# A gated linear attention with an ELU feed-forward layer: the scan input of span 1 loaded ahead of q and k of span 0, and its scan moved behind that of span 0

## The chip, the core and the metric

The kernel runs on one core of one Trainium2 chip. The metric is device time in microseconds (us). The engines are PE (TensorE: matmuls, with its weight loads listed as PEld), DVE (VectorE), ACT (ScalarE), POOL (GpSimd) and SP (SyncE, which here issues the transfers). Each engine works through its own list of instructions in order and waits at an instruction whose inputs are not there yet.

## The reference

```
state = zeros((B, H, D, D))
for t in range(S):
    state = alpha[:, :, t, :, None] * state + einsum('bhd,bhe->bhde', k[:, :, t], v[:, :, t])
    y[:, :, t] = einsum('bhd,bhde->bhe', q[:, :, t], state)
x = y.transpose(0, 2, 1, 3).reshape(B * S, H * D)
h = x @ w_in
g = where(h > 0, h, exp(minimum(h, 0)) - 1)
out = g @ w_out
```

B = 4, H = 8, S = 768, D = 48; w_in is 384 x 2048 and w_out 2048 x 384. All of it is float32 to the caller.

## The kernel before, in words

Time is cut into spans of 128 steps, 6 for each of the 4 batches, 24 in all. Within a span the recurrence becomes matrix products: a running product P of alpha (the scan, with a row of ones in front), its inverse R (by logarithm and exponential), k divided and q multiplied by P, then score, state and output matmuls. Two spans make one block of 256 tokens for the feed-forward layer, whose weights are split into a high and a low part by the engines while the first spans run. After the first 60 us or so the weights are ready and the rest is a steady alternation of spans and feed-forward matmuls.

The order of all work is written by hand: a table of tokens, START, is read from left to right and each token emits its instructions; each engine then holds its own instructions in that order. The tokens that matter here, for span i:

- LA.i loads the alpha part ("a") of the span, 128 x 516 numbers, 258 KB; LB.i loads its k and q, 128 x 1024 numbers, 512 KB, into the same tile `qka`. Both are issued by SP (lines 179 and 183). LV.i loads v, F.f a piece of the weights, L.i all of a later span.
- SC.i is the scan on DVE (line 209): P from a. LN.i and EX.i, both on ACT (lines 218 and 223): R = exp(-ln P). EX also reads out an accumulator, a short instruction of its own.
- KA.i (line 231): k times R, kept in `qka`. It needs EX.i and LB.i; for span 0 it runs on DVE. KB.i (line 236): R = P times R, on DVE for span 0 and on POOL for span 1; it overwrites the R that KA.i reads. KC.i (line 241, DVE): (R - 2) times k, which ends the preparation of k.
- SQ.i (line 258): q times P, on POOL for span 0 and on DVE for span 1. It needs SC.i and LB.i.
- TP.i (line 282, PE): four transposes of k, behind KC.i. KN.i (line 311, ACT) copies them out. S.i (line 346, PE): scores from k and SQ.i's result. U.i (line 392, PE): state update from KN.i's result. UA.i (line 409), UC.i (line 442), UP.i (line 418), MK.i (line 363), YL.i and Y.i (lines 453 and 497), XH.i (line 512) finish the span.
- X.n issues n matmuls on constant data (line 126); 16 of them stand ahead of TP.0.
- DA, DB, DC (lines 581, 587, 593, DVE), WH (line 619, ACT) and WP (lines 628 and 516, PE) split a pair of weights.

The lines on which the steps rest:

```
nc.sync.dma_start(out=qtile(i)[:, 2 * NP * W:], in_=qka[i, :, 2 * NP * W:QW])            # LA
nc.sync.dma_start(out=win[i]["t"][:, 0:2 * NP * W], in_=qka[i, :, 0:2 * NP * W])         # LB
nc.vector.tensor_tensor_scan(out=P..., data0=t[:, 2 * NP * W:], data1=first..., ...)     # SC
eng(KAV, i).tensor_tensor(out=d["kt"], in0=d["kt"], in1=d["R"], op=ALU.mult)             # KA
eng(KBV, i).tensor_tensor(out=d["R"], in0=pw(i), in1=d["R"], op=ALU.mult)                # KB
nc.vector.scalar_tensor_tensor(out=d["kt"], in0=d["R"], scalar=-2.0, in1=d["kt"], ...)   # KC
eng(SQV, i).tensor_tensor(out=st[:, 0], in0=d["q"], in1=pw(i), op=ALU.mult)              # SQ, i < 6
KAV, KBV, SQV = (0, 1, 2, 3, 10), (0, 3, 5, 6), (1, 2, 3, 5)   # spans on DVE; the others on POOL
```

Of the kernel before, what the change touches and what calls it, by code (L numbers as in the profile page):

```python
# [14 lines left out]
B, H, S, D = 4, 8, 768, 48  # L15
# [29 lines left out]


START = """
LA.0 LB.0 SC.0 LN.0 EX.0 LA.1 KA.0 KB.0 LB.1 SC.1 X.2 LV.0 LN.1 X.2 KC.0 F.2 SQ.0 EX.1 F.0 TP.0 KN.0 S.0 U.0
SQ.1 UA.0 KA.1 KB.1 MK.0 L.2 KC.1 UC.0 YL.0 LV.1 TP.1 PC.0 Y3.0 Y.0 KN.1 DA.0 PC.1 LV.2 DB.0 L.3 F.4 S.1 SC.2
U.1 XH.0 F.6 DC.0 UP.1 LN.2 XP.0 EX.2 KA.2 SQ.2 MK.1 UA.1 F.5 WH.0 WP.0 YL.1 F.1 F.3 UC.1 Y3.1 KB.2 SC.3 KC.2  # L50
WH.2 XL.0 PC.2 LN.3 DA.2 EX.3 SQ.3 Y.1 DB.2 KA.3 XH.1 TP.2 WP.2 DC.2 KB.3 KN.2 DA.1 DB.1 XP.1 KC.3 U.2 XL.1
# [916 lines left out]
```

## Time and profile before

| | |
|---|---|
| median of 3 runs | 504.81 us (504.31 to 505.99) |
| the profiled execution | 504.17 us |
| its span in the profile | 502.5 us |
| busy share of the span: PE, PEld, DVE, ACT, POOL | 98%, 95%, 77%, 58%, 26% |
| mean granted clock of TensorE | 0.999 |

Times in the profile count from the span's start, so the profiled execution's own time is its span and some 1.7 us around it. In a row of the timeline the first number is the start, the second the duration, then the engine, the line, the operation and its operands; brackets give the engine's idle time before it and what ended that. A row of transfers gives the tensor, the issuing queue, how many, the size of each and the time from issue to landing.

### The profile page before, as it was taken

The numbers are of one execution on the slowest core, as the hardware profiler recorded it, in microseconds if no ns is written. First come the engines' busy times: TensorE is split into PE (matmuls) and PEld (weight loads), VectorE is DVE, ScalarE is ACT, GpSimd is POOL, SyncE is SP. The second block draws the span as 40 slices with busy tenths as digits, with TensorE's granted clock in tenths as the row PEclk, the third lists the DMA queues.
The fourth block names the chain that finished last, engine by engine and source line by source line (L and its number), as shares of the span: only waits on it lengthen the run. The fifth ranks groups of instructions, "written<-read, shape, count | busy, mean of one in ns | idle before, by whom it ended". The sixth has DMA issues, their size and how long they took to land.

```text
span 502.5 us, 13254 instructions
## 1 busy us (share of the span) xinstructions
PE 492.4 (98%) x5404; PEld 476.0 (95%) x5404; DVE 386.6 (77%) x807; ACT 289.5 (58%) x689; POOL 129.4 (26%) x111
## 2 busy tenths in 40 slices
PE   7999999999999999999999999999999999999996
PEld 3789999999999899999999999999999999999996
DVE  6999999989998579769869969769969978344321
ACT  3656786456460677646745756647755755454432
POOL 4125566443320302501501501501501500000000
PEclk9999999999999999999999999999999999999999
DMA  8999324222521145226135145234332321110001
GB/s 311 412 411 382 91 95 165 64 59 100 190 59 64 57 130 178 65 83 219 54 119 178 48 119 182 63 112 172 82 112 97 95 76 44 56 42 8 3 33 36
DMA packets 22403, 61.13 MB, mean 122 GB/s; under 512 B 2880, under 2 KB 9792, under 8 KB 22336
## 3 DMA queue, kind: packets, MB, share of 16 engines
q1 hardware_dynamic: 22048, 59.83, 35.4%
q8 instruction: 44, 0.72, 0.6%
q10 hardware_dynamic: 288, 0.39, 0.2%
q14 instruction: 23, 0.19, 0.1%
HBM read 53.53 MB, written 4.72 MB: 116 GB/s over the span
## 4 chain that ended last, share of the span: by engine, by line
PE 96%; DVE 2%; ACT 1%; issue 1%; ACTq 0%
PE o L706 40%; PE h L655 40%; PE y L458 4%; PE y L453 2%; PE q L374 2%; PE q L330 2%; PE u L392 1%; PE sc L346 1%; PE wp L126 1%; PE y L497 1%; PE tp L282 1%; DVE kn L292 0%; PE yl L453 0%; PE wd L628 0%; DVE st L358 0%
## 5 line engine op out<-in xcount | busy, mean ns | idle before, releaser
L655 PE MATMUL h<-xt,w 128*128 128x256 f32 x1728 | 215.0, 282 | 0.0
L655 PEld LDWEIGHTS h<-xt,w 128*128 128x128 f32 x1728 | 209.3, 188 | 1.8
L706 PE MATMUL o<-w,gh 128*128 128x384 f32 x768 | 199.3, 341 | 0.6 <-ACT gh L679 0.6
L706 PEld LDWEIGHTS o<-w,gh 128*128 128x128 f32 x768 | 136.9, 188 | 1.6 <-ACT gh L679 0.8
L706 PE MATMUL o<-w,gl 128*128 128x384 f32 x384 | 130.0, 339 | 0.1
L679 ACT CAST gh<-h 128x512 fp32r<-128x512 f32 x96 | 55.9, 583 | 79.6 <-DVE h L673 39.3
L692 DVE TENSOR_TENSOR gl<-h,gh 128x512 fp32r<-128x512 f32 x96 | 65.5, 687 | 35.5 <-ACT gh L679 34.2
L292 DVE STREAM_TRANSPOSE kn<-qka 32x128 f32<-32x128 f32 x288 | 87.0, 302 | 4.5
L663 ACT ACTIVATE r<-h 128x512 f32<-128x512 f32 x96 | 57.0, 595 | 47.2 <-PE h L655 40.7
L673 DVE SCALAR_TENSOR_TENSOR h<-r,h 128x512 f32<-128x512 f32 x96 | 64.6, 689 | 16.9 <-ACT r L668 16.1
L706 PEld LDWEIGHTS o<-w,gl 128*128 128x128 f32 x384 | 72.1, 188 | 0.4 <-DVE gl L692 0.4
L231 POOL TENSOR_TENSOR qka<-qka,R 128x512 f32<-128x512 f32 x19 | 26.1, 1375 | 164.6 <-DVE gl L692 127.6
L668 ACT ACTIVATE r<-r 128x512 f32<-128x512 f32 x96 | 59.4, 631 | 0.7
L261 POOL TENSOR_TENSOR st<-qka,P 64x512 f32<-64x512 f32 x36 | 42.8, 1189 | 21.7 <-DVE P L209 16.2
L358 DVE TENSOR_TENSOR st<-q,mask 64x256 f32<-64x256 f32 x72 | 30.4, 422 | 12.0 <-ACT vs L409 9.2
L209 DVE TENSOR_TENSOR_SCAN P<-qka,first 128x516 f32<-128x516 f32 x24 | 30.6, 1275 | 1.6 <-DMA qka<-in_qka_dram 1.2
L236 POOL TENSOR_TENSOR R<-P,R 128x512 f32<-128x512 f32 x20 | 24.2, 1211 | 27.3 <-DVE qka L231 25.9
L218 ACT ACTIVATE R<-P 128x512 f32<-128x512 f32 x24 | 15.2, 632 | 27.8 <-DVE P L209 27.8
L411 DVE TENSOR_TENSOR vs<-vs,q 48x192 f32<-48x192 f32 x30 | 10.5, 350 | 19.1 <-PE q L330 16.9
L511 ACT ACTIVATE y<-y 128x128 fp32r<-128x128 f32 x20 | 5.5, 275 | 30.0 <-PE y L458 26.6
L639 POOL TENSOR_TENSOR w<-spare,w 128x768 fp32r<-128x768 f32 x7 | 15.8, 2256 | 26.0 <-ACT w L619 13.9
L611 ACT ACTIVATE ck<-ck,lim 128x384 f32<-128x384 f32 x32 | 20.6, 644 | 0.1
(101 smaller groups left out, 425.7 us busy)
## 6 DMA issues: line engine op xcount, KB each, us to landing
qka<-in_qka_dram SPq DMA_DIRECT2D x22, 770.0 KB, 6.5
raw<-in_wgt_dram SPq DMA_DIRECT2D x16, 768.0 KB, 12.3
ck<-in_wgt_dram SPq DMA_DIRECT2D x32, 384.0 KB, 3.2
vs<-in_vv_dram SPq DMA_DIRECT2D x36, 192.0 KB, 4.3
out_dram<-ot SPq DMA_DIRECT2D x22, 192.0 KB, 1.9
vs<-in_vv_dram SPq DMA_DIRECT2D x6, 384.0 KB, 11.6
xt<-y SPq DMA_DIRECT2D x40, 48.0 KB, 2.3
qka<-in_qka_dram SPq DMA_DIRECT2D x2, 512.0 KB, 5.0
```

Source lines behind the costliest of these rows:

```text
L209: nc.vector.tensor_tensor_scan(out=P.rearrange("p n w -> p (n w)"), data0=t[:, 2 * NP * W:], data1=first.rearrange("p n w -> p (n w)"), in ...
L231: eng(KAV, i).tensor_tensor(out=d["kt"], in0=d["kt"], in1=d["R"], op=ALU.mult)
L261: eng(SQV, i).tensor_tensor(out=st[r, a], in0=d["q"][r], in1=pw(i)[r], op=ALU.mult)
L292: nc.vector.transpose(out=kn[32 * t:32 * t + 32, :, 32 * g:32 * g + 32], in_=d["kt"][32 * g:32 * g + 32, :, 32 * t:32 * t + 32])
L358: nc.vector.tensor_tensor(out=d["st"][r, a, :, c * C:(c + 1) * C], in0=d["s4"][a][o], in1=mask[o].unsqueeze(1).broadcast_to([64, NP, C]), ...
L655: nc.tensor.matmul(h[:, f, :], lhsT=t[:, wi, ws], rhs=x[:, c, xi, :], start=(f == 0 and k == 0), stop=(k == 8), skip_group_check=True)
L663: nc.scalar.activation(out=r, in_=d["h"], func=AF.Relu, scale=-1.0)
L668: nc.scalar.activation(out=d["r"], in_=d["r"], func=AF.Exp, scale=-1.0)
L673: nc.vector.scalar_tensor_tensor(out=d["h"], in0=d["r"], scalar=-1.0, in1=d["h"], op0=ALU.add, op1=ALU.max)
L679: nc.scalar.copy(out=gh, in_=d["h"])
L692: nc.vector.tensor_tensor(out=gl, in0=d["h"], in1=d["gh"].bitcast(F32), op=ALU.subtract)
L706: nc.tensor.matmul(o[:, 0:DM], lhsT=gt[:, f, ms], rhs=t[:, wi, f * DM:f * DM + DM], start=(j == 0 and f == 0 and k == 0), stop=(j == NJ - ...
```

## The change

One row of START is written in another order. LA.1 moves from behind EX.0 to directly behind LA.0, SC.1 from behind LB.1 to directly behind EX.0, and LN.1 with it. Nothing is added or removed, and every instruction stays on its engine.

```
 START = """
-LA.0 LB.0 SC.0 LN.0 EX.0 LA.1 KA.0 KB.0 LB.1 SC.1 X.2 LV.0 LN.1 X.2 KC.0 F.2 SQ.0 EX.1 F.0 TP.0 KN.0 S.0 U.0
+LA.0 LA.1 LB.0 SC.0 LN.0 EX.0 SC.1 LN.1 KA.0 KB.0 LB.1 X.2 LV.0 X.2 KC.0 F.2 SQ.0 EX.1 F.0 TP.0 KN.0 S.0 U.0
 SQ.1 UA.0 KA.1 KB.1 MK.0 L.2 KC.1 UC.0 YL.0 LV.1 TP.1 PC.0 Y3.0 Y.0 KN.1 DA.0 PC.1 LV.2 DB.0 L.3 F.4 S.1 SC.2
```

The engines' own lists differ in two places only. SP's list at its beginning (qka_123 is the tile of span 0, qka_124 that of span 1; 128x516 is a, 128x1024 is k and q):

```order
 L964 UNCONDITIONAL_BRANCH
 L179 DMA qka_123<-in_qka_dram 128x516
+L179 DMA qka_124<-in_qka_dram 128x516
 L183 DMA qka_123<-in_qka_dram 128x1024
-L179 DMA qka_124<-in_qka_dram 128x516
 L183 DMA qka_124<-in_qka_dram 128x1024
 L191 DMA vs_105<-in_vv_dram 128x768
```

The load of a of span 1 has moved past the load of k and q of span 0; all later loads keep their places.

DVE's list, from its last setup instruction to SQ.1 (the rows of line 209 are SC.0 and SC.1, then KA.0, KB.0, KC.0):

```order
 L110 TENSOR_SCALAR minus<-ident 128x128
 L209 SCALAR_TENSOR_TENSOR P<-qka_123,first 128x516
+L209 SCALAR_TENSOR_TENSOR P<-qka_124,first 128x516
 L231 TENSOR_TENSOR qka_123<-qka_123,R 128x512
 L236 TENSOR_TENSOR R<-P,R 128x512
-L209 SCALAR_TENSOR_TENSOR P<-qka_124,first 128x516
 L241 SCALAR_TENSOR_TENSOR qka_123<-R,qka_123 128x512
 L258 TENSOR_TENSOR st<-qka_124,P 128x512
```

SC.1 has moved past KA.0 and KB.0, so that KC.0 follows KB.0 directly. ACT's list is the same as before (LN.0, EX.0, LN.1, EX.1), and so are those of PE and POOL.

## The prediction

> **What bounds the kernel now.** I read the page first, then the chain of waits, then the timeline of the first 22 us, where the change lies, and the landing times of the first transfers. On the page and in the busy time by stage:
>
> ```profile
> PE 492.4 (98%) x5404; PEld 476.0 (95%) x5404; DVE 386.6 (77%) x807; ACT 289.5 (58%) x689; POOL 129.4 (26%) x111
> PE 96%; DVE 2%; ACT 1%; issue 1%; ACTq 0%
> 9.54:22.40 12.86, 11.86 (x225) 9.48 (x225) 11.93 (x15) 6.94 (x19) 2.73 (x2) 1.00 1.02 415
> 22.40:62.00 39.60, 39.60 (x591) 37.18 (x591) 37.70 (x43) 26.11 (x58) 17.20 (x8) 1.00 0.83 308
> ```
>
> PE (the first column behind the length) sets the end: from 22.4 us to 62 it has no idle time at all. So a delay of PE before 22.4 us is never made up, and a gain lasts only as far as no operand comes late. What PE waits for before 22.4 us stands in the chain:
>
> ```profile
> 2.08 5.78 PE wp L126 x16
> 7.86 1.68 issue
> 9.54 0.63 PE tp L282 x4
> 19.22 0.83 ACT w L619
> 20.09 0.44 PE wd L516
> ```
>
> The constant matmuls end at 7.86, and PE then waits 1.68 us for TP.0. The change acts on that wait. What TP.0 waits for, from the timeline:
>
> ```profile
> 3.61 1.23 DVE L209 TENSOR_TENSOR_SCAN P<-qka,first 128x516 f32<-128x516 f32 x1 [0.72 <-DMA qka<-in_qka_dram]
> 5.21 1.18 POOL L258 TENSOR_TENSOR st<-qka,P 128x512 f32<-128x512 f32 x1 [0.86 <-DMA qka<-in_qka_dram]
> 6.08 0.19 ACT L223 ACTIVATION_READ_ACCUMULATOR R<-R 128x1 f32 x1
> 6.30 0.69 DVE L231 TENSOR_TENSOR qka<-qka,R 128x512 f32<-128x512 f32 x1 [1.45 <-ACT R L223]
> 7.02 0.69 DVE L236 TENSOR_TENSOR R<-P,R 128x512 f32<-128x512 f32 x1
> 7.63 1.23 DVE L209 TENSOR_TENSOR_SCAN P<-qka,first 128x516 f32<-128x516 f32 x1
> 8.77 0.67 DVE L241 SCALAR_TENSOR_TENSOR qka<-R,qka 128x512 f32<-128x512 f32 x1
> ```
>
> These are SC.0, SQ.0, the end of EX.0, KA.0, KB.0, SC.1, KC.0. DVE idles 1.45 us before KA.0 (4.84 to 6.30), and SC.1 stands between KB.0 and KC.0. SQ.0 runs on POOL inside DVE's idle time.
>
> **The change part by part.** *The scan.* SC.1 moves into DVE's idle time: 4.84 + 1.23 = 6.07, before EX.0 ends (6.27). KC.0 then follows KB.0 by 0.03 us, as KB.0 follows KA.0 (6.99 to 7.02), and ends at 7.71 + 0.03 + 0.67 = 8.41 instead of 9.44: 1.03 us gained if nothing else moved. For that the a of span 1 must be there by 4.84 us. LN.1 and EX.1 stay behind EX.0 on ACT and cost nothing there; ACT idles until TP.0 is read out.
>
> *The loads.* 258 KB move ahead of q and k of span 0. Four rows in the order of their issue at 0.82, 1.27, 1.74 and 2.21 us (a of span 0, q and k of span 0, a of span 1, q and k of span 1), the last number being the time to landing:
>
> ```profile
> 0.82 0.39 SPq L179 DMA_DIRECT2D qka<-in_qka_dram  x1
> 2.21 0.43 SPq L183 DMA_DIRECT2D qka<-in_qka_dram  x1
> ...
> qka<-in_qka_dram SPq DMA_DIRECT2D x1, 258.0 KB, 2.7
> qka<-in_qka_dram SPq DMA_DIRECT2D x1, 512.0 KB, 3.8
> qka<-in_qka_dram SPq DMA_DIRECT2D x1, 258.0 KB, 5.4
> qka<-in_qka_dram SPq DMA_DIRECT2D x1, 512.0 KB, 6.2
> ```
>
> They landed at 3.52, 5.07, 7.14 and 8.41. In the new order a of span 1 is second and has 516 KB up to its end, less than the 770 KB that were there at 5.07: it lands between 3.6 and 5.1, so SC.1 is hardly held. But q and k of span 0 are third, with 1028 KB up to their end, exactly the place at which the third transfer landed at 7.14. Two things are read from what had moved up to a time:
>
> ```profile
> DMA packets 189, 0.45 MB, mean 128 GB/s; under 512 B 16, under 2 KB 16, under 8 KB 189
> DMA packets 290, 0.79 MB, mean 181 GB/s; under 512 B 26, under 2 KB 26, under 8 KB 290
> DMA packets 419, 1.06 MB, mean 204 GB/s; under 512 B 41, under 2 KB 41, under 8 KB 419
> DMA packets 446, 1.15 MB, mean 209 GB/s; under 512 B 46, under 2 KB 46, under 8 KB 446
> DMA packets 509, 1.39 MB, mean 223 GB/s; under 512 B 46, under 2 KB 46, under 8 KB 509
> ```
>
> These count from 0 to 3.5, 4.4, 5.2, 5.5 and 6.25 us. First, a lower end: the 770 KB (0.79 MB) of the first two transfers had moved by 4.4 us, 0.7 us before the second landed, and the 1028 KB (1.05 MB) of three by 5.2, so the third is there at 5.9 at the earliest. Second, the packets under 512 bytes tell between the ends. They come 16 to a transfer (16 when the first has landed), one for each of 16 engines as I read them. At 5.5 us 46 of 48 were through for three transfers, and then none came for 0.75 us: two engines were late with the third transfer by over 1 us. If an engine stalls at a time, or at a place in its list, the third transfer pays whichever it is. I take 7.1, near its own row, and keep 5.9 to 8.4 (when all four had landed) for the range. [...]
>
> *What becomes of KA.0 and SQ.0.* Both need q and k of span 0 (KA.0 reads k, SQ.0 q). Before, these were there at 5.07, SQ.0 ran in DVE's idle time, and KA.0 waited for EX.0 alone. At 7.1 both are released together, on two engines. What that costs is shown where POOL and DVE meet elsewhere:
>
> ```profile
> 43.27 2.25 DVE L593 SCALAR_TENSOR_TENSOR wm<-raw,wm 128x1536 int32<-128x1536 int32 x1
> 43.86 2.83 POOL L231 TENSOR_TENSOR qka<-qka,R 128x512 f32<-128x512 f32 x1
> 46.76 1.19 POOL L236 TENSOR_TENSOR R<-P,R 128x512 f32<-128x512 f32 x1
> 47.10 1.95 DVE L209 TENSOR_TENSOR_SCAN P<-qka,first 128x516 f32<-128x516 f32 x1
> 66.23 1.29 POOL L231 TENSOR_TENSOR qka<-qka,R 128x512 f32<-128x512 f32 x1
> ```
>
> Line 231 on POOL takes 1.29 us alone (66.23) and 2.83 when a DVE operation with two SBUF operands, started before it, still has 1.66 us to run: it waits 1.54 of these. The scan takes 1.95 instead of 1.23 when it starts 0.85 us before POOL's end. Whichever starts second waits until about 0.12 us before the other's end. KA.0, KB.0, KC.0, the scan and SQ.0 are all of that kind. [...]
>
> *The sum.* DVE reacted to a landing in 0.09 us (3.52 to 3.61), POOL in 0.14 (5.07 to 5.21), so KA.0 starts first, at 7.2, and ends at 7.9. SQ.0 is waiting and enters 0.12 us before that, at 7.78, and needs 1.18: 8.96. KB.0 waits for KA.0 anyway, so it comes second, enters at 8.84 and ends at 9.53; KC.0 runs from 9.56 to 10.23. TP.0 started 0.10 us behind KC.0 (9.44 to 9.54): 10.33, which is **0.8 us later** than 9.54. That loss passes down: the scores, UA.0, UC.0 and DA.0 all follow TP.0, and with them
>
> ```profile
> 13.24 0.96 DVE L581 TENSOR_SCALAR wm<-raw 128x1536 int32<-128x1536 int32 x1
> 17.06 1.73 DVE L593 SCALAR_TENSOR_TENSOR wm<-raw,wm 128x1536 int32<-128x1536 int32 x1
> 18.38 0.19 ACT L223 ACTIVATION_READ_ACCUMULATOR R<-R 128x1 f32 x1
> 18.99 0.33 ACT L409 ACTIVATE vs<-u 128x192 f32<-128x192 f32 x1 [0.43 <-PE u L418]
> 23.22 0.96 DVE L581 TENSOR_SCALAR spare<-raw 128x1536 int32<-128x1536 int32 x1 [0.51 <-DMA raw<-in_wgt_dram]
> ```
>
> The wait of WP.0 for WH.0 at 20.09 moves by the same, since WH.0 starts behind UA.1, which waits for PE at 18.99. DVE's 0.51 us of idle time at 23.22 gives DVE some back, but PE has none there. The profiled execution becomes 504.17 + 0.8 = 504.97; it lies 0.64 us under the median of the runs shown, so the median becomes 504.81 + 0.8 = **505.6**.
>
> *A cap on any gain.* The last of the weights that DA.0 needs was issued second of two, at some 3.7 us:
>
> ```profile
> 3.16 1.00 SPq L565 DMA_DIRECT2D raw<-in_wgt_dram  x2
> raw<-in_wgt_dram SPq DMA_DIRECT2D x1, 768.0 KB, 9.4
> ```
>
> so it lands at 13.1, and no transfer ahead of them is added or taken away. DA.0 can come forward by 0.1 us only (13.24 to 13.13), and DC.0's end from 18.79 to 18.68. EX.2's end (18.57) comes forward by the same 0.1, so UA.1 starts at 18.46 at the earliest and WH.0 0.23 us behind it, as it does now: 18.7 instead of 19.22. Of the 1.03 us at most **0.5** reaches PE at 20.09.
>
> **The rivals.**
>
> *1. q and k land early, a small gain.* At 5.9 to 6.0 SQ.0 waits for SC.1 and enters at 5.95, ending at 7.13. KA.0 enters at 7.01 and ends at 7.70, KB.0 at 8.42, KC.0 at 9.12, TP.0 starts at 9.22: 0.3 us gained, 504.5. For it: the two late engines may be the stall of one execution. Against: the lag did not come back with the fourth transfer (8.41). The two cases meet where TP.0 is at 9.54, with q and k landing at about 6.35.
>
> *2. They land late, but the engines do not get in each other's way.* KA.0 at 7.2, KC.0 ends at 9.27, TP.0 at 9.37: 0.2 us gained, 504.6. Against it are the five rows above.
>
> *3. q and k land last, clearly slower.* If the early transfers finish together rather than one after the other, q and k of span 0 land at 8.4, as those of span 1 did. Everything in the sum moves by 1.3: TP.0 at 11.6, 2.1 us lost, 506.9. From a landing at 7.8 on the loss is over 1.5 us. Against it: the four landed in the order of issue, over 1.2 us apart each.
>
> *4. The scan does not fit its gap.* If the stall hits a of span 1 instead, it lands near 5.7, SC.1 runs to 7.0 and holds POOL too; SQ.0 then enters at 6.9 (q and k being there) and KA.0 at 7.95: TP.0 at 10.15, 0.6 us lost, 505.4. That is the change not doing what it says.
>
> **How the numbers follow.** The forecast has 0.50, rival 1 has 0.28, rival 2 has 0.09, rival 3 has 0.06, rival 4 has 0.07. About 0.3% (1.5 us) is what a measurement of this kernel can tell from no change; the runs shown lie 1.7 us apart. Only rival 3 leaves that bound for sure. The forecast leaves it upward with one run in fifteen or so by the spread of the runs (0.04), and a gain of 0.5 needs another 1 us of luck (0.03). So faster 0.03, same 0.87, slower 0.10. The range reaches from the full cap with a low run (504.31 - 0.4 = 503.9) to the forecast with a high one (505.6 + 0.8 = 506.4). The likeliest case alone, with landings from 6.7 to 7.4, gives 505.2 to 505.9.
>
> **What would show it.** SC.1 directly behind SC.0, near 4.9 us, shows the move. The bracket of KA.0 tells the case: a wait that ends with a DMA, near 7.2, is the forecast; one that ends with ACT at 6.3, and a KA.0 longer than 0.69 us, is rival 1. A KB.0 of some 1.5 us with SQ.0 beside it shows the collision. The wait of PE before TP.0 should be 2.4 to 2.5 us instead of 1.68, DA.0 should start near 14 us, and PE should have no idle time behind 23 us. A KC.0 that ends before 9.4 us proves the forecast's sign wrong; a q and k that land before 6.3 us shows that the landing was the step that failed, and a later landing with a KB.0 of 0.69 us that the collision was.

## The result and the profile after

The change made the kernel slower: 510.28 us, median of 5 runs (508.78 to 510.78), against 505.29 for the kernel before in the same comparison, a ratio of 1.0089 with a 95% interval of 1.0066 to 1.0112. The forecast was 505.6, no change. Twelve further executions of the same kernel, run later, had a median of 508.25 (504.55 to 510.62) and a ratio of 1.0043 (1.0014 to 1.0073). The two intervals just overlap; why executions of one kernel differ so much is a part of what follows. The profiled execution took 510.28 us, its span 508.6.

First the page of the changed kernel: busy time, and the granted clock of TensorE in 40 slices of 12.7 us.

```profile
PE 497.5 (98%) x5404; PEld 480.1 (94%) x5404; DVE 390.1 (77%) x807; ACT 289.3 (57%) x689; POOL 128.4 (25%) x111
PEclk9699999999999999999999999999999999999999
```

PE has the same 5404 matmuls and 5.1 us more busy time, so most of the loss is matmuls that took longer. The 6 in the second slice (12.7 to 25.4 us) says why. Now the part that the prediction worked out, in the timeline of the changed kernel:

```profile
2.08 5.99 PE L126 MATMUL wp<-first 128*128 128x512 bf16 x16 [2.08 <-DVE first L120]
3.61 2.36 DVE L209 TENSOR_TENSOR_SCAN P<-qka,first 128x516 f32<-128x516 f32 x2 [0.72 <-DMA qka<-in_qka_dram]
7.45 0.69 DVE L231 TENSOR_TENSOR qka<-qka,R 128x512 f32<-128x512 f32 x1 [1.49 <-DMA qka<-in_qka_dram]
7.50 1.68 POOL L258 TENSOR_TENSOR st<-qka,P 128x512 f32<-128x512 f32 x1 [3.16 <-DMA qka<-in_qka_dram]
8.18 1.55 DVE L236 TENSOR_TENSOR R<-P,R 128x512 f32<-128x512 f32 x1
9.76 0.69 DVE L241 SCALAR_TENSOR_TENSOR qka<-R,qka 128x512 f32<-128x512 f32 x1
10.55 1.09 PE L282 MATMUL tp<-ident,qka 128*128 128x128 f32 x4 [2.49 <-issue]
11.57 1.97 PE L346 MATMUL sc<-st,qka 48*64 48x64 f32 x32
13.47 2.00 PE L392 MATMUL u<-vs,kn 128*64 128x48 f32 x29
21.96 1.27 PE L392 MATMUL u<-vs,kn 128*64 128x48 f32 x32
```

SC.0 and SC.1 run back to back as ordered. KA.0 waits for q and k, which land at 7.3. SQ.0 starts 0.05 us after it, KB.0 takes 1.55 us beside SQ.0, and TP.0 starts at 10.55: 1.01 us later than before. All of that was forecast, with 0.8. What was not: TP.0 takes 1.09 us instead of 0.63, the scores 1.97 instead of 1.15, and U.1 (the last row) starts at 21.96 instead of 16.84. Before, the work from TP.0 to U.1 took 16.84 - 9.54 = 7.30 us; now it takes 11.41. So 5.12 us are lost by U.1, 1.01 by the late start and 4.11 by slower matmuls. In the rest of the program some 1.0 us more were lost in small waits: 0.43 by the scores of span 4, where PE waits at 66.58 for DVE, and some 0.55 in pieces of less than 0.15. Of the profiles of the experiments below, all eight in which U.1 is late by 0.9 us or more lose 0.4 us at that place, and the three in which it is late by 0.2 at most (experiments 3, 9 and 10) lose nothing there. So a late start of 1 us costs some 1.4 by the end of that step.

### The profile page after: what moved, and what is told of

It reads as the page before. It is cut to its first block, busy times and chain, and to the rows that moved or that the text cites. A ratio compares the mean times of both kernels' runs of the same rounds, so it can differ in the third digit from the quotient of the medians.

```text
span 508.6 us, 13253 instructions
## 1 busy us (share of the span) xinstructions
PE 497.5 (98%) x5404; PEld 480.1 (94%) x5404; DVE 390.1 (77%) x807; ACT 289.3 (57%) x689; POOL 128.4 (25%) x111
## 4 chain that ended last, share of the span: by engine, by line
PE 84%; DMA 8%; DVE 4%; issue 1%; ACT 1%; POOL 0%; SPq 0%; DVEq 0%; POOLq 0%
PE o L706 39%; PE h L655 36%; DMA raw<-in_wgt_dram 7%; PE y L458 4%; PE q L374 2%; PE q L330 2%; DMA qka<-in_qka_dram 1%; PE sc L346 1%; PE y L453 1%; DVE gl L692 1%; DVE P L209 1%; DVE h L673 1%; DVE spare L581 1%; DVE kn L292 0%; POOL st L258 0%
## 5 line engine op out<-in xcount | busy, mean ns | idle before, releaser
L209 DVE TENSOR_TENSOR_SCAN P<-qka,first 128x516 f32<-128x516 f32 x24 | 32.0, 1335 | 1.2 <-DMA qka<-in_qka_dram 0.7
```

The costliest lines, as they stand in the source:

```text
L209: nc.vector.tensor_tensor_scan(out=P.rearrange("p n w -> p (n w)"), data0=t[:, 2 * NP * W:], data1=first.rearrange("p n w -> p (n w)"), in ...
```

## The clock

The busy time by stage, with the granted clock in the third column from the right (1.00 is full speed), for four stretches of 0.1 us of the changed kernel:

```profile
10.20:10.30 0.10, 0.00 (x0) 0.00 (x0) 0.10 (x1) 0.00 (x0) 0.00 (x0) 1.00 1.47 614
10.30:10.40 0.10, 0.00 (x0) 0.00 (x0) 0.10 (x2) 0.00 (x0) 0.00 (x0) 0.53 0.58 246
20.40:20.50 0.10, 0.10 (x8) 0.10 (x6) 0.10 (x1) 0.00 (x0) 0.00 (x0) 0.50 0.90 369
20.50:20.60 0.10, 0.10 (x8) 0.10 (x6) 0.10 (x1) 0.00 (x0) 0.00 (x0) 0.78 1.06 430
```

The clock falls to a half within the second row: 0.53 is a full clock for 0.006 us and half for the rest, so at 10.30, while PE still waits for TP.0. It is back within the fourth row, at 20.54. That is 10.24 us at half speed, and nearly all of PE's work from TP.0 up to the scores of span 1 (at 20.89) lies in it.

Theory A: the late start cost 1.0 us, and PE's idle time, grown from 1.68 to 2.49 us, cost the clock. Theory B: the transfers or the late weights are what costs, whatever the clock does.

## The experiments

Each is the kernel named with one edit. Granted clocks are means over the whole program; about 0.990 is 10 us at half speed (0.990 with 10.24 us in the profile of the change), 0.993 is 7 us (0.993 with 6.83 us in that of experiment 2). A half clock of 3.4 us lowers the mean by 0.003 (0.997 in the profile of experiment 4), and in the profile of the kernel before the clock is also at a half at the very end (501.4 to 502.5 us; the mean is 0.999). From the 3.41 us of experiment 4 I estimate that a low end lowers the mean by up to 0.003. So a mean of 0.996 to 1.0 doesn't rule out one short fall, and "fell" below means 0.995 or less or a fall seen in the profile.

**1. The change with PE kept busy.** Ten more constant matmuls.

```
-... LB.1 X.2 LV.0 X.2 KC.0 ...
+... LB.1 X.2 LV.0 X.12 KC.0 ...
```

> The change, with ten more constant matmuls (26 instead of 16) ahead of TP.0, so that PE is busy until about 10.2 us and idles only 0.3 to 0.5 us before TP.0. Theory A (the late start of TP.0 costs 1.0 us, and the rest of the loss, 4.1 us up to U.1, is TensorE's granted clock, which falls to 0.50 at 10.3 us after 2.2 us without a matmul and stays there until 20.5): the clock stays at 1.00, TP.0 starts near 10.55 as in the change, U.1 starts near 17.9 instead of 21.96, and the time is 1.0 to 1.6 us above the kernel before, 505.9 to 506.9. Theory B (the early transfers and the late weights are what costs, the clock follows): the time stays near that of the change, 509 to 511, with PE waiting for weights before 22 us.

Measured: 506.14 us, median of 10 executions, ratio 1.0041 (1.0012 to 1.0071). From its timeline:

```profile
8.32 1.55 DVE L236 TENSOR_TENSOR R<-P,R 128x512 f32<-128x512 f32 x1
10.70 0.63 PE L282 MATMUL tp<-ident,qka 128*128 128x128 f32 x4 [1.24 <-issue]
18.00 1.27 PE L392 MATMUL u<-vs,kn 128*64 128x48 f32 x32
```

TP.0 starts as late as in the change, the four transposes take 0.63 us again, and U.1 starts at 18.00, as theory A had it (17.9). Transfers, collision and late start are all still there; only the clock is back, and 4 us with it. Two of the ten executions still showed a clock of 0.988, at 510.9 and 511.1.

**2. The kernel before with less to keep PE busy.** Four constant matmuls fewer, nothing else.

```
-WARM = 12
+WARM = 8
```

> The kernel before, with 12 instead of 16 constant matmuls, all loads and all of DVE's order as before. TP.0 starts at 9.54 as before, but PE is idle from about 6.9 us. Theory A: the clock falls to 0.50 within that idle time, by 9.2 us, and stays there for about 10 us, so U.1 starts near 20.9 instead of 16.84 and the time is 3.5 to 5 us above the kernel before, 509 to 510. Theory B: nothing that the loads or DVE do has changed, so the time is that of the kernel before, 504.5 to 505.8.

Measured: 509.0 us, median of 4, ratio 1.0087 (1.0071 to 1.0104); all four at 0.990 to 0.993. Beside it the kernel before had 505.06. Its timeline and two stretches of its clock:

```profile
9.59 0.63 PE L282 MATMUL tp<-ident,qka 128*128 128x128 f32 x4 [2.21 <-issue]
10.15 1.52 PE L346 MATMUL sc<-st,qka 48*64 48x64 f32 x32
...
10.70:10.80 0.10, 0.10 (x10) 0.10 (x6) 0.10 (x1) 0.10 (x1) 0.00 (x0) 0.68 0.73 307
17.50:17.60 0.10, 0.10 (x6) 0.10 (x8) 0.10 (x1) 0.00 (x0) 0.00 (x0) 0.69 0.76 307
```

Loads and DVE's order are those of before, TP.0 starts on time, and 3.9 us are lost, against 5.0 in the change, where 1.0 is the late start. Theory B falls with these two runs. One thing does not fit the expectation: the clock fell at 10.74, when PE was at work again for 1.1 us, and not within the idle time. So it does not answer to the idle time as it passes. It was low for 6.83 us here and for 10.24 in the change: 2 and 3 times 3.41. So U.1 started at 19.56 and not at 20.9.

**3. The change without the collision.** SQ.0 goes to DVE, behind KC.0.

```
-WLV, KAV, KBV, SQV = (0, 4), (0, 1, 2, 3, 10), (0, 3, 5, 6), (1, 2, 3, 5)
+WLV, KAV, KBV, SQV = (0, 4), (0, 1, 2, 3, 10), (0, 3, 5, 6), (0, 1, 2, 3, 5)
```

> The change, with SQ.0 on DVE behind KC.0 instead of on POOL beside KA.0. KA.0 still waits for q and k until about 7.4. Theory A: KB.0 takes 0.69 us instead of 1.55, KC.0 ends near 9.6, TP.0 starts near 9.7, PE idles 1.6 to 1.7 us, the clock stays at 1.00, S.0 waits a little for SQ.0 (10.3), and the time is within 0.5 us of the kernel before: 504.8 to 505.8. Theory B: the time stays above 508, since the loads are those of the change. If KB.0 still takes 1.5 us, the collision of POOL and DVE was not what held it.

Measured: 504.71 us, median of 10 (503.7 to 510.29), ratio 1.0008 (0.9982 to 1.0033). From its timeline:

```profile
6.83 0.69 DVE L231 TENSOR_TENSOR qka<-qka,R 128x512 f32<-128x512 f32 x1 [0.82 <-ACT R L218]
7.55 0.69 DVE L236 TENSOR_TENSOR R<-P,R 128x512 f32<-128x512 f32 x1
9.07 0.63 PE L282 MATMUL tp<-ident,qka 128*128 128x128 f32 x4 [1.01 <-issue]
```

KB.0 takes 0.69 us, so the 0.86 more of the change was SQ.0 beside it. In this execution q and k landed at 6.7. That, too, makes TP.0 early: of its 1.48 us against the change (10.55), 0.6 are the landing and 0.86 the collision. Nine executions lay between 503.7 and 506.0, the tenth at 510.29 with a clock of 0.990. With the collision gone the change is no slower than before, and it is not measurably faster either.

**4. The wanted part without the load.** The loads as before, KC.0 ahead of SC.1.

```
-LA.0 LB.0 SC.0 LN.0 EX.0 LA.1 KA.0 KB.0 LB.1 SC.1 X.2 LV.0 LN.1 X.2 KC.0 F.2 SQ.0 EX.1 ...
+LA.0 LB.0 SC.0 LN.0 EX.0 LA.1 KA.0 KB.0 KC.0 LB.1 SC.1 X.2 LV.0 LN.1 X.2 F.2 SQ.0 EX.1 ...
```

> The kernel before with its order of loads, and KC.0 moved ahead of SC.1 on DVE: the wanted part of the change (KC.0 directly behind KB.0) without the moved load. q and k land near 5.1, KA.0 starts at 6.3, KC.0 ends near 8.4, TP.0 starts near 8.5 and PE idles 0.6 us. Theory A: PE gains 1.0 us at TP.0, of which at most 0.5 is left at 20 us, because DA.0 waits for its weights until 13.1; 504.3 to 505.3, to be read in the profile rather than in the time. Theory B says the same of the start; if the gain is lost altogether, something else than DA.0 holds PE before 20 us.

Measured: 506.67 us, median of 10, ratio 1.0031 (1.0009 to 1.0053): a miss. From its timeline, and its clock in three stretches of 0.1 us:

```profile
8.66 0.63 PE L282 MATMUL tp<-ident,qka 128*128 128x128 f32 x4 [0.51 <-issue]
9.22 1.15 PE L346 MATMUL sc<-st,qka 48*64 48x64 f32 x32
11.03 0.56 ACT L311 COPY kn<-tp 128x512 f32<-128x512 f32 x1
11.64 1.20 PE L392 MATMUL u<-vs,kn 128*64 128x48 f32 x29 [1.28 <-ACT kn L311]
...
13.80:13.90 0.10, 0.08 (x4) 0.02 (x1) 0.10 (x2) 0.10 (x2) 0.00 (x0) 0.94 1.13 461
17.20:17.30 0.10, 0.10 (x7) 0.10 (x6) 0.10 (x1) 0.00 (x0) 0.00 (x0) 0.50 1.21 492
17.30:17.40 0.10, 0.10 (x8) 0.10 (x6) 0.10 (x1) 0.00 (x0) 0.00 (x0) 1.00 0.75 308
```

TP.0 comes 0.9 us early, but KN.0 stands behind EX.1 on ACT, and EX.1 now follows a later scan; U.0 waits 1.28 us for KN.0 and starts 0.5 us later than before. My expectation had looked at DVE and PE and not at ACT. And the clock fell in this execution too, from 13.89 to 17.30: 3.41 us. Four of the ten had 0.990 to 0.994 and took 506.65 to 509.04. So the median holds both losses, and the run doesn't say what the order of DVE alone is worth.

**What the lengths say.** Low stretches of 3.41, 6.83 and 10.24 us are 1, 2 and 3 times 3.41 us; I read that as a clock that is set for stretches of 3.41 us. The full-speed time between two low ones agrees: in the changed kernel it runs from 20.54 to 508.65 us, 143.0 times 3.413 (a third of 10.24). The borders differ from execution to execution: the low time of the changed kernel began at 10.30 in one profile and at 11.76 in another (experiment 11). Waits of PE of 2.0 to 2.5 us stood ahead of three of the falls: 2.49 in the change, 2.21 in experiment 2, 2.00 in experiment 6.

**5. No collision, and PE kept busy.** Experiment 3 with X.6 for the second X.2 (20 constant matmuls).

```
-... LV.0 X.2 KC.0 ...      (of experiment 3)
+... LV.0 X.6 KC.0 ...
```

> The change, with SQ.0 on DVE behind KC.0 (as in the run before with that edit) and four more constant matmuls (20), so that PE idles some 0.2 us instead of 1.0 before TP.0 at about 9.1. Theory A (time and granted clock both follow PE's idle time before 10 us): no execution falls to a mean clock of 0.990, so the single execution of 510.3 seen without the fill does not come back; all lie between 503.7 and 506, median 504.2 to 505.0, at or up to 0.8 us below the kernel before. Theory B (the early loads are what costs at times, by their landing): executions near 510 come back at the same rate, one in ten.

Measured: 504.8 us, median of 12 (503.57 to 508.04), ratio 0.9993 (0.9974 to 1.0013). Two of twelve were at 0.991 and 0.995, 507.9 and 508.0, against the expectation. The profiled execution was one of them: q and k landed at 7.6, TP.0 started at 9.98, and PE idled 1.91 us in spite of the fill, whose matmuls came 0.21 us apart from 5.05 on (0.43 before that) and ended at 8.06.

**6. The kernel before with one constant matmul less.** WARM = 11.

> The kernel before with one constant matmul less (15), so that PE idles some 1.9 us before TP.0 instead of 1.68; nothing else differs. Theory A with a limit on idle time within stretches of 3.4 us (the clock fell after 2.2 us of idle time in two kernels and did not after 1.7): between the limits, so part of the executions fall to a clock of 0.990 to 0.993 and 508 to 510 us and part stay at 504.2 to 506. Theory C (it needs a full 2.2 us without a matmul): all stay at the time of the kernel before. Theory B: all stay there too.

Measured: 504.99 us, median of 12, ratio 1.0018 (0.9992 to 1.0044), in two groups: eight at 504.3 to 506.9 (seven of them up to 505.1) with clocks of 0.996 to 1.0, four at 508.7 to 510.1 with 0.987 to 0.993. That is the split that theory A expected, from 0.3 us of idle time. The profiled execution fell:

```profile
9.62 0.90 PE L282 MATMUL tp<-ident,qka 128*128 128x128 f32 x4 [2.00 <-issue]
6.42:9.83 3.41, 1.41 (x8) 0.58 (x7) 3.38 (x5) 0.83 (x2) 0.05 (x1) 1.00 1.02 390
9.84:20.07 10.23, 9.97 (x132) 8.46 (x132) 7.35 (x9) 3.51 (x10) 1.18 (x1) 0.50 1.02 418
```

**7. The moved load alone.** a of span 1 ahead of q and k of span 0, DVE as before.

```
-LA.0 LB.0 SC.0 LN.0 EX.0 LA.1 KA.0 KB.0 LB.1 SC.1 ...
+LA.0 LA.1 LB.0 SC.0 LN.0 EX.0 KA.0 KB.0 LB.1 SC.1 ...
```

> The moved load alone: a of span 1 is loaded ahead of q and k of span 0, and SC.1 stays between KB.0 and KC.0 as before. Theory A (the load is the harmful half, the moved scan the useful one): KA.0 waits for q and k until 7.0 to 7.5, KB.0 takes 1.5 us beside SQ.0 and ends near 9.7, SC.1 then runs to 10.9 and KC.0 ends at 11.5 to 11.6, TP.0 starts near 11.7, 1.1 us later than in the change; PE idles 3.6 us, the clock falls as in the change, and the time is 0.8 to 1.5 us above the change: 511 to 512. Theory B (moving the scan is harmful by itself): no slower than the change, 510 or less.

Measured: 510.75 us, median of 5, ratio 1.011 (1.0087 to 1.0133); four at 510.4 to 511.6 with 0.987 to 0.990, one at 505.95 with 1.0. The load alone is slower than before by as much as the whole change; whether it is slower than the change, as expected, is not resolved (0.5 us between medians of runs that spread by 2). The profiled execution was the one that did not fall, and tells most about the clock. q and k landed early in it, at 6.2, so KA.0 hardly waited for them and TP.0 started at 10.47, not at the 11.7 expected. The collision is there all the same:

```profile
6.39 1.70 POOL L258 TENSOR_TENSOR st<-qka,P 128x512 f32<-128x512 f32 x1 [2.04 <-DMA qka<-in_qka_dram]
7.09 1.55 DVE L236 TENSOR_TENSOR R<-P,R 128x512 f32<-128x512 f32 x1
10.47 0.63 PE L282 MATMUL tp<-ident,qka 128*128 128x128 f32 x4 [2.69 <-issue]
6.30:9.71 3.41, 1.48 (x7) 0.49 (x5) 3.31 (x4) 0.03 (x1) 1.70 (x1) 1.00 1.02 401
```

PE idles 2.69 us, more than in the change, at a full clock. The record of the clock in the trace starts at 6.30 in this execution (ahead of it the views print 1.00, though the constant matmuls there come 0.43 us apart and not 0.21 as later). So that stretch ends at 9.71 if it lasts 3.41 us (as that of the change did, from 6.89 to 10.30), within the idle time: 1.93 us of it lie in that stretch and 0.76 in the next. In experiment 6 all 2.00 us lay in one stretch, and it fell.

**8. The change with the idle time filled.** X.16 for the second X.2 (30 constant matmuls).

> The change with fourteen more constant matmuls (30), which fill PE's idle time before TP.0 nearly to the end (about 10.4 us). Theory A: the two executions in ten near 511 that were left with 26 matmuls (1.2 us idle) are gone, the mean clock is 0.997 or more in all, and the median is 1.0 to 1.5 us above the kernel before, 505.9 to 506.6: the late start of TP.0 without the clock. Theory B: executions near 511 come back.

Measured: 506.1 us, median of 12 (504.84 to 506.94), ratio 1.0011 (0.9993 to 1.0028); clocks from 0.997 to 1.0, none fell. Its median lies 0.9 us over that of the runs of before beside it (505.22). But that is not the lateness of the change alone. In the profiled execution, the slowest of the twelve (506.94), the 30 matmuls themselves held TP.0 up. KC.0 ended at 10.80, so TP.0 could have started at 10.9:

```profile
2.08 9.56 PE L126 MATMUL wp<-first 128*128 128x512 bf16 x30 [2.08 <-DVE first L120]
11.48 0.60 PE L282 MATMUL tp<-ident,qka 128*128 128x128 f32 x4
```

**9. No collision, 24 constant matmuls.** Experiment 3 with X.10 for the second X.2.

> The change, with SQ.0 on DVE behind KC.0 and eight more constant matmuls (24). Theory A, now in this form: the granted clock is set for stretches of 3.41 us, whose borders lie elsewhere in each execution, and it falls for the next stretch when PE did too little in the last one. With 20 matmuls two executions in twelve fell, when q and k landed late (PE idle 1.9 us before TP.0). With 24 the idle time is at most about 1 us even then, so none falls (mean clock 0.996 or more in all), and the median is 504.2 to 505.2, at the kernel before or up to 0.8 us below. Theory B (the early loads by themselves cost at times): executions at 508 and more come back.

Measured: 505.6 us, median of 12 (504.35 to 507.45), ratio 0.9998 (0.9978 to 1.0018); none fell (0.997 to 1.0). The median is 0.4 over the expected band: with this fill no execution fell in twelve, and nothing is gained over before. The slowest, 507.45, had a clock of 0.999, so not every slow execution is a fall.

**10. The kernel before with 22 constant matmuls.** X.8 for the second X.2.

> The kernel before with six more constant matmuls (22), so that PE idles 0.4 to 0.8 us before TP.0 instead of 1.68; nothing else differs. Theory A: the few executions of the kernel before with a clock of 0.987 to 0.993 (2 of the 54 so far, at 508.6 and 509.5) do not come back, and the median stays that of the kernel before within 0.5 us, since TP.0 is held by KC.0. If the median falls by over 0.5 us, the idle time cost something else as well.

Measured: 505.01 us, median of 12, ratio 0.9992 (0.9972 to 1.0012); one of twelve at 508.23 with 0.993. The median is as expected, the rare fall is not gone. Where it happened isn't known, since the profiled execution did not fall.

**11. The change again.**

> The change once more, unaltered, for the share of its executions in which the clock falls. Theory A: PE idles 2.0 to 2.6 us in a stretch of 3.41 us wherever its border lies but for a border in the middle of the idle time, so nine in ten or more show a mean clock of 0.987 to 0.993 and 508.5 to 511 us; the few that do not lie at 505.5 to 507, the time of the change without the clock. Theory B (late weights): no such split, all between 509 and 511 whatever the clock.

Measured: 508.25 us, median of 12. Seven fell (507.3 to 510.6, clocks 0.987 to 0.993), five did not (504.55 to 506.26, median 505.62, clocks 0.997 to 1.0). The split is as expected. Both groups begin about 1 us lower than expected, and the share is another: 7 of 12 where I had nine in ten. With the five runs of the first comparison, all of which fell, it is 12 of 17. The first comparison had more falls than the later one, and by these counts that is most of the difference between the two ratios. The profiled execution fell at another time than the first one, after a longer wait:

```profile
2.08 5.02 PE L126 MATMUL wp<-first 128*128 128x512 bf16 x16 [2.08 <-DVE first L120]
10.96 0.63 PE L282 MATMUL tp<-ident,qka 128*128 128x128 f32 x4 [3.86 <-DVE qka L241]
...
8.35:11.76 3.41, 0.80 (x12) 0.66 (x14) 3.34 (x5) 0.13 (x1) 1.23 (x1) 1.00 1.03 425
11.77:22.00 10.23, 9.97 (x148) 8.79 (x145) 7.36 (x8) 3.62 (x11) 1.18 (x1) 0.50 1.02 409
```

The same 16 constant matmuls ended at 7.10 here and at 8.07 in the first profile. The clock's record starts at 4.94 here and at 6.89 there, and until about then the constant matmuls come 0.43 us apart, later 0.21. So where that start lies also decided how long these 16 constant matmuls lasted. With q and k landing at 7.7 instead of 7.33, PE idled 3.86 us instead of 2.49, in the same program.

## When the clock falls

PE's busy time within the stretch after which the clock was set. Borders of fallen stretches are read from the clock as above, those of the others are an estimate, counted in steps of 3.41 us from the start of the clock's record.

| kernel | stretch, us | PE busy in it, us | next stretch |
|---|---|---|---|
| change | 6.89 to 10.30 | 1.17, constant matmuls | half |
| 11 (change again) | 8.35 to 11.76 | 0.80, TP.0 and scores | half |
| 2 (before, 12 matmuls) | 7.33 to 10.74 | 1.19, mostly TP.0 and scores | half |
| 6 (before, 15 matmuls) | 6.42 to 9.84 | 1.41, mostly constant matmuls | half |
| 7 (load alone) | 6.30 to 9.71 | 1.48, constant matmuls | full |
| before (16 matmuls) | 6.48 to 9.89 | 1.72, constant matmuls and TP.0 | full |
| 4 (KC.0 first) | 10.48 to 13.89 | 1.85, U.0 and YL.0 | half |
| 5 (no collision, 20 matmuls) | 8.56 to 11.97 | 1.99, TP.0, scores, U.0 | half |
| 1 (change, 26 matmuls) | 8.76 to 12.16 | 2.16, constant matmuls, TP.0, scores | full |
| 10 (before, 22 matmuls) | 8.63 to 12.04 | 2.29, TP.0, scores, U.0 | full |
| 3 (no collision, 16 matmuls) | 6.88 to 10.28 | 2.39, constant matmuls, TP.0, scores | full |

Each row is one execution. Where constant matmuls (128 x 128 by 512 columns) made up most of the stretch, 1.41 us of the 3.41 were too little (1.2 of them constant matmuls, 0.2 TP.0) and 1.48 were enough. With TP.0 and the span's small matmuls (48 to 128 rows by 48 or 64 columns) alone, 1.99 us were not enough and 2.29 were. So busy time as the profile has it does not tell the two outcomes apart (1.48 us held, 1.99 fell). The two kinds differ in their rows, in the columns and in the number type (bf16 and f32); which of these counts was not separated. The slow return would fit: in the change PE was busy for 9.68 of 10.20 us at half clock, and it took three stretches. That too is argued and not tested.

## Why the prediction was wrong

- **The landing of q and k of span 0: right.** Forecast 7.1 by its place in the order, measured 7.33. Over the eight profiles with this order of loads it ranged from 6.2 (experiment 7) to 7.7 (8 and 11), inside the bounds of 5.9 to 8.4. It is not a fixed place, as my argument from the packet counts had it.
- **The collision: right.** KB.0 with SQ.0 beside it was forecast to end 1.63 us after KA.0; it ended 1.59 after it (8.14 to 9.73); KB.0 took 1.55 us instead of 0.69, SQ.0 1.68 instead of 1.18. Experiment 3 shows it by taking it away.
- **TP.0: right in kind.** +0.8 forecast, +1.01 measured in the first profile and +1.42 in that of experiment 11, where q and k landed later. The time of the executions that did not fall lies 0.3 us over the kernel before beside them in experiment 11 (505.62, five executions) and 0.9 in experiment 1 (506.0, eight executions, with more constant matmuls). The forecast lies between. That 505.62 is so near to the forecast 505.6 is luck, since the kernel before stood at 505.28 there and not at 504.81.
- **The wait of PE: right by luck.** 2.49 us fits the forecast to the hundredth because two things made up for each other: TP.0 came 0.2 us later than forecast, and the constant matmuls ended 0.21 later than before (8.07 for 7.86). In experiment 11 it was 3.86.
- **The cap of 0.5 on a gain** agrees with the profile of experiment 3, where TP.0 came 0.47 early: DA.0 started at 13.15, 0.1 early, WH.0 at 18.75 where 18.7 was the forecast limit, and WP.0 behind it at 19.63, 0.46 early. In the time of the whole program that gain is not resolved. Rival 2's sum leaves out the gaps between DVE's instructions; with them KC.0 ends at 9.31, which changes nothing.
- **The step that failed: "That loss passes down".** It took the durations behind TP.0 from the kernel before and let them move as a block. I had forecast PE's wait at "2.4 to 2.5 us instead of 1.68", measured 2.49, and drew nothing from it but lateness. The runs showed in its place that the longer wait, in 12 of 17 executions, costs a half clock for two or three stretches of 3.41 us: 4.1 us by U.1 in the profiled one. DA.0, which was forecast near 14 us, started at 16.34. The same step missed the 0.43 us at the scores of span 4; I had expected no idle time of PE behind 23 us. None of the four rivals had it, though the constant matmuls ahead of TP.0 were in the chain of waits that I quoted, and the idle time that they left was the very number that the change moved.
- **The range** (503.9 to 506.4) held the executions that did not fall and none of the others; the chance of 0.10 for slower was rival 3 and noise, for another reason.
- **The trace of before could not show a half clock at that place**, but it held a hint: 1.68 us of idle time with the clock at 1.00 said only that 1.68 was safe in that execution, and I extended it to 2.5 without a row. It also showed that PE's pace was not fixed: the weight loads of the constant matmuls came 0.43 us apart up to 6.33, then five in 1.04 us.

```profile
5.90 0.15 PEld L126 LDWEIGHTS <-first 128*128 128x128 bf16 x1 [0.28 <-issue]
6.33 1.04 PEld L126 LDWEIGHTS <-first 128*128 128x128 bf16 x5 [0.28 <-issue]
```

## What to carry to other kernels

When a change lengthens a wait of TensorE, price not only the lateness but the clock behind it (here 1.01 and 4.11 us by U.1): look how long PE idles or does small work within 3.4 us, and whether the trace shows the clock holding after a wait of that length. Early in a program, matmuls on constant data that end just before the first real one can go with a clock that holds (experiment 9: PE idle 0.32 us in the profile, no fall in twelve). Too many hold up the first real one instead (experiment 8: TP.0 at 11.48 where 10.9 was possible), and how long they last differs between executions (16 of them 5.02 us in experiment 11, 5.99 in the first profile of the same kernel); when the work they lead up to moves, they have to be counted again. And when a load is moved forward, ask whom it delays, and which two engines will then be released by the same landing: SQ.0 was free in DVE's idle time and made KB.0 0.86 us longer as soon as both waited for one transfer.

## What the runs showed of the hardware that I had not expected

- The granted clock changed at borders a multiple of 3.41 us apart (low stretches of 3.41, 6.83 and 10.24 us). They lay elsewhere in two profiles of the same kernel (the change fell at 10.30 and at 11.76), and a fall came when PE was already at work again (10.74 us in experiment 2, 1.1 us after TP.0).
- One constant matmul less, 0.3 us more of idle time (2.00 for 1.68), put 4 of 12 executions of the kernel before 4 us higher, while its median did not move. A median of few executions near such a wait says little; the split by clock says more.
- The kernel before falls too, rarely: 3 of the 83 executions beside the experiments had a clock of 0.987 to 0.993 (508.5 to 509.5 us). Its wait, 1.68 us in the profile, is 0.3 us short of the one that fell in experiment 6, and even with 22 constant matmuls one of twelve fell; the reason for those is open. So is that of five more of the 83: two took 508.7 and 509.3 us with a clock of 0.996, three 507.2 to 507.7 with 0.998 or 0.999.
- The constant matmuls came 0.43 us apart at first and 0.21 from some time between 4.94 and 8.02 us on, by the profiles, so that 16 of them took 5.02 to 6.07 us in the same place of the program.
